# Tying the late weight conversions on VectorE behind the sum that precedes them in the program

## The chip, the cores and the metric

The kernel runs on one core of a Trainium2 chip. The metric is the device time of one execution in microseconds. The kernel before takes 1346.18 us, the median of three runs (1344.56 to 1347.51).

## What is computed

An attention over 4 batches, 12 heads, 448 positions and 64 channels, with an RMS norm on queries and keys, is followed by two feed-forward layers over the 1792 tokens that come out of it (768 wide, 2048 hidden). All weights arrive as float64.

```python
attn = softmax(rmsnorm(q, g_q) @ rmsnorm(k, g_k).T / sqrt(64)) @ v   # per batch and head
x = attn.transpose(0, 2, 1, 3).reshape(1792, 768)
h = x @ w_in;   r = max(h, 0);  x = (s * (r * r) + b) @ w_out         # layer 0
h = x @ w_in2;  g = h * cos(h); out = g @ w_out2                      # layer 1
```

## The kernel before

Every product of the layers is made of three TensorE products of float32 halves, so each operand is split into a high and a low part (`halves`, lines 379 to 383: ACT copies the high part, GpSimd or VectorE subtracts it).

The work runs in stages. Attention, pair of heads by pair of heads, runs beside layer 0 for the first two batches. Then come three passes over the hidden width, each in eight steps p: the pass (0,1) is layer 0 for the last two batches, the passes (1,0) and (1,1) are layer 1 for the first and the last two. A step has a `phase_in` (seven products of a Strassen scheme, with sums on VectorE at lines 767 and 772) and a `phase_out` (six output tiles of `unit_out_1` in layer 0, seven of `unit_out_2` in layer 1). An output tile is accumulated over the steps: its first visit is a copy on ACT (lines 530 and 554), each later one a VectorE sum of PSUM into the accumulator (lines 532 and 556). In the pass (0,1) `phase_out` of p stands in the program behind `phase_in` of p + 1, and so in the other passes.

`convert` (lines 385 to 413) turns one 128 x 384 block of float64 weights into float32: a DMA loads the raw block (lines 393 and 396, tile `raw`, two buffers), ACT makes `c` (line 402, two buffers) and `t` (line 403, three buffers), VectorE runs three operations in the order of the program: L406 puts the sign into `t`, L407 clips `c`, L408 joins both. For all but one kind of weight a DMA then stores the block (line 411, `wd`), and `prepare_in` and `prepare_out` load it from there and split it when its step comes.

The 64 blocks of layer 1 are the late ones (`late=True`). The last loop of the kernel places them: beside the steps of the passes (0,1) and (1,0) it adds to a credit, and at each whole credit one conversion is written into the program.

```python
            if calm:
                conversion(5.8 / 13 if q_ == passes[0] else 5 / 14)
```

The place in the program is not the place on an engine. The framework's scheduler lists each engine's instructions: it takes what is ready by its own model of time, the earlier one in the program first, and each engine then runs its list in order. A DMA is issued by SP in the order of its list as well. `issue_after(later, earlier)` adds an edge within one engine: the later instruction is listed behind the earlier one. It adds no semaphore.

Of the kernel before, what the change touches and what calls it, by code (L numbers as in the profile page):

```python
# [15 lines left out]
ALU = mybir.AluOpType  # L16
# [17 lines left out]
def body(ctx, tc, q, k, v, g_q, g_k, w1_in, w1_out, s_in, b_in, w2_in, w2_out, out):  # L34
    nc = tc.nc
# [43 lines left out]
    marks = {}  # L79
# [5 lines left out]
    def issue_after(later, earlier):  # L85
        info = mybir.DependencyInfo(mybir.DependencyClass.NoSync, mybir.DependencyReason.DATA)
        tc.add_manual_dep(later.ins, earlier.ins.name, info, reason="issue order")
# [12 lines left out]
    def products(w, x):  # L100
        return ((w[0], x[0]), (w[1], x[0]), (w[0], x[1]))
# [268 lines left out]
    def tile_of(ck, f):  # L370
        return ck + NCK * f
# [13 lines left out]
    def convert(layer, kind, a, e, o, gate=None, late=False):  # L385
        w = ((w1_in, w1_out), (w2_in, w2_out))[layer][kind]
        kk = f"{layer}_{kind}_{a}_{e}_{o}"
        own = late or count["raw"] % 3 < 2
        raw = (wp if own else pools["att"]).tile([P, CW], I64, tag="raw", name=f"raw_{kk}", bufs=2 if own else 1)
        count["raw"] += 1  # L390
        if kind == 0:
            src = w[o * CW:(o + 1) * CW, a * P:(a + 1) * P].rearrange("(c p) f -> p c f", p=P)
            dma = nc.sync.dma_start(raw.rearrange("p (c f) -> p c f", f=P), src)
        else:
            ft = tile_of(a, o)
            dma = nc.sync.dma_start(raw, w[ft * P:(ft + 1) * P, e * CW:(e + 1) * CW])
        ru = raw.bitcast(U32).rearrange("p (n two) -> p n two", two=2)
        lo, hi = ru[:, :, 0], ru[:, :, 1]
        c = wp.tile([P, CW], U32, tag="c", name=f"c_{kk}", bufs=2)
        cf = c.bitcast(F32)  # L400
        t = wp.tile([P, CW], U32, tag="t", name=f"t_{kk}", bufs=3)
        for z in (nc.scalar.activation(cf, hi.bitcast(F32), AF.Copy, scale=2.0**-112),  # L402
                  nc.scalar.activation(t, lo, AF.Copy, scale=LSCALE, bias=-0.5)):  # L403
            if gate is not None:
                issue_after(z, gate)
        nc.vector.scalar_tensor_tensor(t, hi, 0x80000000, t, ALU.bitwise_and, ALU.bitwise_or)  # L406
        nc.vector.tensor_scalar(cf, cf, VMAX, -VMAX, ALU.min, ALU.max)  # L407
        nc.vector.scalar_tensor_tensor(t, c, 3, t, ALU.logical_shift_left, ALU.bitwise_or)  # L408
        if (layer, kind) != (0, 1):
            d = dram.tile([P, CW], F32, tag=f"w_{kk}", name=f"wd_{kk}")  # L410
            nc.sync.dma_start(d, t.bitcast(F32))
            plain[layer, kind, a, e, o] = d
        return dma, t.bitcast(F32)
# [95 lines left out]
    def po_tile(key):  # L509
        if "psb" in pools:  # L510
            return pools["psb"].tile([P, 2, 512], F32, tag="po", name=f"po_{key}", bufs=2)
        return pools["psm"].tile([P, 512], F32, tag="mo", name=f"po_{key}", bufs=2)

    def unit_out_1(w, ck, et, bs):
        key = f"0_{ck}_{et}_{bs[0]}_{len(bs)}"
        cols = slice(et % (NE // 2) * P, (et % (NE // 2) + 1) * P)
        pr = bs[0] // 2
        po = po_tile(key)
        po = po[:, :len(bs), :S] if "psb" in pools else po[:, :S].unsqueeze(1)
        for k, b in enumerate(bs):  # L520
            for f in range(CF):
                for n, (a, m) in enumerate(products([z[:, cols] for z in w[f]], g[tile_of(ck, f), b])):
                    nc.tensor.matmul(po[:, k, :], a, m, start=(f == 0 and n == 0), stop=(f == CF - 1 and n == 2))  # L523
            visits[et, b] = visits.get((et, b), 0) + 1
        if (0, pr) not in acc:
            acc[0, pr] = ac.tile([P, 2 * NE * S], F32, tag="acc", name=f"acc_0_{pr}")
        n = (2 * et + bs[0] % 2) * S
        at = acc[0, pr][:, n:n + len(bs) * S].rearrange("p (k s) -> p k s", s=S)
        if visits[et, bs[0]] == 1:
            nc.scalar.copy(at, po)  # L530
            return
        nc.vector.tensor_tensor(at, po, at, ALU.add)  # L532
        if visits[et, bs[0]] < NCK:
            return
        for k, b in enumerate(bs):
            t = dram.tile([P, S], F32, tag=f"y_{b}_{et}", name=f"yd_{b}_{et}")
            nc.sync.dma_start(t, at[:, k, :])
            stash[1, b, et] = t

    def unit_out_2(w, pr, ck, t):  # L540
        key = f"1_{ck}_{pr}_{t}"
        j0 = t * P
        po = po_tile(key)[:, :, :EH]
        for eh in range(2):
            for f in range(CF):
                x = [z[:, j0:j0 + P] for z in g[tile_of(ck, f), "pair", pr]]
                for n, (a, m) in enumerate(products(x, w[eh][f])):
                    nc.tensor.matmul(po[:, eh, :], a, m, start=(f == 0 and n == 0), stop=(f == CF - 1 and n == 2))  # L548
        if (1, pr) not in acc:
            acc[1, pr] = ac.tile([P, NT * E], F32, tag="acc", name=f"acc_1_{pr}")  # L550
        rows_at = acc[1, pr][:, t * E:(t + 1) * E]
        at = rows_at.rearrange("p (k e) -> p k e", k=2)
        if ck == 0:
            nc.scalar.copy(at, po)
        else:
            nc.vector.tensor_tensor(at, po, at, ALU.add)  # L556
        if ck < NCK - 1:
            return
        j = j0
        while j < j0 + P:  # L560
            b, c, p = 2 * pr + j // S, j % S // CP, j % CP
            n = min(CP - p, j0 + P - j)
            rows = out[b * S:(b + 1) * S, :].rearrange("(p c) e -> c p e", c=NCH)[c, p:p + n, :]
            nc.sync.dma_start(rows, rows_at[j - j0:j - j0 + n, :])
            j += n
# [177 lines left out]
    def phase_in(layer, pr, p):  # L743
        w, x = late_w["in", layer, pr, p], late_x[layer, pr]
        key = f"{layer}_{pr}_{p}"
        pairs = []
        for f in range(CF):
            n = count["g"]
            count["g"] += 1
            gp, nb = (ma, 3) if n % 4 < 3 else (pools["lt"], 1)  # L750
            pairs.append([gp.tile([P, 2, S], F32R, tag=f"g{z}", name=f"g{z}_{key}_{f}", bufs=nb) for z in "hl"])
            for b in range(2):
                g[tile_of(p, f), 2 * pr + b] = [z[:, b, :] for z in pairs[f]]
            g[tile_of(p, f), "pair", pr] = [z.rearrange("p b s -> p (b s)") for z in pairs[f]]

        def bank(what):
            return pools["psb"].tile([P, 512], F32, tag="ph", name=f"ph_{key}_{what}", bufs=4)[:, :S]

        def product(at, a, b, first):
            wb = [z.rearrange("p (c f) -> p c f", f=P) for z in w[a]]  # L760
            for c in range(NE // 2):
                for n, (z, m) in enumerate(products([z[:, c, :] for z in wb], x[b, c])):
                    nc.tensor.matmul(at, z, m, start=(first and c == 0 and n == 0), stop=(c == NE // 2 - 1 and n == 2), skip_group_check=not first)  # L763

        def combine(what, at, u):
            t = temp("u", f"{what}_{key}", 3)
            nc.vector.tensor_tensor(t, at, u, ALU.add)
            return t

        def result(f, b, h, u=None, into=None):  # L770
            if u is not None:
                nc.vector.tensor_tensor(into, h, u, ALU.add)
                h = into
            epilogue_in_bank(layer, f"{key}_{f}_{b}", h, *(z[:, b, :] for z in pairs[f]))

        pa = bank("a")
        product(pa, "11", "11", True)
        p1 = temp("u", f"p1_{key}", 3)
        nc.scalar.copy(p1, pa)
        yield  # L780
        pb = bank("b")
        product(pb, "s2", "2", True)
        u2 = combine("u2", pb, p1)
        yield
        product(pa, "12", "21", False)
        result(0, 0, pa)
        yield
        pc = bank("c")
        product(pc, "s3", "3", True)
        u3 = combine("u3", pc, u2)  # L790
        yield
        pd = bank("d")
        product(pd, "s1", "1", True)
        result(1, 1, pd, u3, pb)
        yield
        product(pc, "22", "4", False)
        result(1, 0, pc, u2, pc)
        yield
        product(pd, "s4", "22", False)
        result(0, 1, pd, u2, pd)  # L800
        yield
# [132 lines left out]
```

## Time and profile before

| | |
|---|---|
| median of three runs | 1346.18 us |
| the profiled execution | 1347.68 us, span 1345.7 us |
| mean granted TensorE clock | 0.973 |
| busy: PE, DVE, ACT, POOL | 91%, 73%, 58%, 43% of the span |
| sums L532 into two banks at once, pass (0,1) | first start 688.1 us, last 878.6 us |
| sums L556, first of the pass (1,0) | 943.0 us |

PE is TensorE's matmuls, DVE is VectorE, POOL is GpSimd, SP issues the DMAs. The busy times are shares of the whole span. A stretch view gives them for one stage, with the granted clock. In a timeline the bracket tells how long the engine was idle before and what released it.

### The profile page before, as it was taken

How to read it: one execution, taken by the hardware profiler on the slowest of the kernel's cores; microseconds unless marked ns; L12 is line 12 of the kernel's file. 1: busy time of each engine (PE TensorE's matmuls, PEld its weight loads, DVE VectorE, ACT ScalarE, POOL GpSimd, SP SyncE). 2: the span in 40 equal slices, each digit the busy share in tenths (PEclk: the TensorE clock that was granted, in tenths of full speed). 3: DMA queues.
4: the chain of work that ended last, by engine and by line, in shares of the span. 5: the costliest groups of instructions: out<-in, count | busy, mean ns of one | idle time of the engine just before them, and what ended most of it. 6: DMA issues, size and time to landing. Idle time of an engine off the chain costs nothing.

```text
span 1345.7 us, 19429 instructions
## 1 busy us (share of the span) xinstructions
PE 1229.1 (91%) x6408; PEld 1008.1 (75%) x6408; DVE 978.1 (73%) x1539; ACT 784.6 (58%) x1749; POOL 578.7 (43%) x647
## 2 busy tenths in 40 slices
PE   5999998989899899865988989979999989999998
PEld 2555665767667676754877779869999979999998
DVE  5889769677767765899778886675766785576665
ACT  4778767655566554535766666457655653754451
POOL 3566538443353431465333335545655641111120
PEclk9999999999999899987999999989999989999999
DMA  3323325534343331776776775374444537433432
GB/s 103 111 85 122 118 74 184 160 117 138 107 157 105 105 108 57 238 278 207 245 228 229 247 243 185 131 253 153 171 158 135 189 96 233 149 124 106 130 118 82
DMA packets 152068, 207.83 MB, mean 154 GB/s; under 512 B 15872, under 2 KB 141984, under 8 KB 151968
## 3 DMA queue, kind: packets, MB, share of 16 engines
q1 hardware_dynamic: 151968, 206.60, 47.9%
q8 instruction: 50, 0.82, 0.3%
q14 instruction: 50, 0.41, 0.1%
HBM read 139.30 MB, written 67.24 MB: 153 GB/s over the span
## 4 chain that ended last, share of the span: by engine, by line
PE 47%; DVE 20%; ACT 11%; DMA 10%; issue 6%; POOL 5%; SPq 0%; POOLq 0%; ACTq 0%; DVEq 0%
PE po L548 15%; PE po L523 8%; DMA raw<-in_moe_w_in_dram 5%; DVE t L406 5%; PE ph_a L763 4%; ACT pr L230 4%; PE av L271 3%; PE ph_c L763 3%; PE sc L210 3%; PE ph_d L763 3%; PE ph L494 2%; DVE t L408 2%; PE ph_b L763 2%; PE tp L248 2%; DMA raw<-in_moe_w_out_dram 2%
## 5 line engine op out<-in xcount | busy, mean ns | idle before, releaser
L383 POOL TENSOR_TENSOR wl_o<-wl_o,wh_o 128x384 fp32r<-128x384 f32 x64 | 68.0, 1074 | 241.8 <-ACT wh_o L380 241.8
L548 PE MATMUL po<-wh_o,gh 128*128 128x384 f32 x448 | 151.9, 339 | 6.5 <-DVE acc L556 6.3
L230 ACT ACTIVATE pr<-sc,top 112x448 f32<-112x448 f32 x184 | 116.2, 634 | 69.6 <-DVE top L222 69.3
L548 PE MATMUL po<-wh_o,gl 128*128 128x384 f32 x448 | 150.6, 336 | 0.0
L548 PE MATMUL po<-wl_o,gh 128*128 128x384 f32 x448 | 148.5, 336 | 0.0
L556 DVE TENSOR_TENSOR acc<-po,acc 128x768 f32<-128x768 f32 x98 | 93.4, 954 | 55.0 <-PE po L548 54.8
L402 ACT ACTIVATE c<-raw 128x384 f32<-128x384 f32 x128 | 71.3, 557 | 101.7 <-DMA raw<-in_moe_w_in_dram 41.6
L248 PEld LDWEIGHTS tp<-ident,pr 112*112 112x112 f32 x768 | 78.5, 134 | 69.5 <-issue 13.4
L222 DVE TENSOR_REDUCE top<-sc 112x1 f32<-112x448 f32 x192 | 112.8, 616 | 23.7 <-PE sc L210 22.9
L532 DVE TENSOR_TENSOR acc<-po,acc 128x448 f32<-128x448 f32 (+1 forms) x126 | 97.0, 773 | 38.0 <-PE po L523 37.6
L406 DVE SCALAR_TENSOR_TENSOR t<-raw,t 128x384 uint32<-128x384 uint32 x128 | 103.6, 810 | 26.1 <-ACT t L403 23.9
L407 DVE TENSOR_SCALAR c<-c 128x384 f32<-128x384 f32 x128 | 69.6, 545 | 64.0 <-ACT c L402 63.6
L248 PE MATMUL tp<-ident,pr 112*112 112x112 f32 x768 | 102.6, 266 | 13.2 <-ACT pT L254 5.3
L210 PE MATMUL sc<-kT,qT 64*112 64x448 f32 x384 | 99.4, 595 | 0.9 <-DVE kT L201 0.9
L523 PE MATMUL po<-gh,wh_o 128*128 128x448 f32 x192 | 73.8, 386 | 25.5 <-DVE acc L532 13.7
L383 POOL TENSOR_TENSOR wl<-t,wh 128x384 fp32r<-128x384 f32 x64 | 68.4, 1076 | 61.8 <-ACT wh L380 60.5
L408 DVE SCALAR_TENSOR_TENSOR t<-c,t 128x384 uint32<-128x384 uint32 x128 | 92.5, 726 | 1.9
L548 PEld LDWEIGHTS po<-wh_o,gh 128*128 128x128 f32 x448 | 84.6, 189 | 10.4 <-DVE acc L556 8.9
L523 PE MATMUL po<-gh,wh 128*128 128x448 f32 x192 | 77.6, 405 | 11.7 <-ACT r L459 7.4
L548 PEld LDWEIGHTS po<-wh_o,gl 128*128 128x128 f32 x448 | 84.7, 189 | 1.4
L548 PEld LDWEIGHTS po<-wl_o,gh 128*128 128x128 f32 x448 | 84.5, 189 | 0.4
L271 PE MATMUL av<-pT,rawv 112*64 112x448 f32 x384 | 79.5, 548 | 0.2 <-DVE pT L252 0.2
(175 smaller groups left out, 3480.3 us busy)
## 6 DMA issues: line engine op xcount, KB each, us to landing
raw<-in_moe_w_in_dram SPq DMA_DIRECT2D x64, 384.0 KB, 3.7
raw<-in_moe_w_out_dram SPq DMA_DIRECT2D x64, 384.0 KB, 3.4
wd<-t SPq DMA_DIRECT2D x96, 192.0 KB, 3.6
wl_o<-wd SPq DMA_DIRECT2D x64, 192.0 KB, 2.4
rd<-wh SPq DMA_DIRECT2D x56, 192.0 KB, 1.9
rd<-wl SPq DMA_DIRECT2D x56, 192.0 KB, 1.9
wl<-wd SPq DMA_DIRECT2D x48, 192.0 KB, 3.2
wh_o<-rd SPq DMA_DIRECT2D x32, 192.0 KB, 3.8
```

The costliest lines, as they stand in the source:

```text
L210: mm.append(nc.tensor.matmul(sc[j], st[i]["qT"][half, c * CP:(c + 1) * CP], st[i]["kT"][half, :], start=True, stop=True))
L222: line("DVE", nc.vector.tensor_reduce(tops[j], sc[j], axis=AX.X, op=ALU.max, negate=True))
L230: e = line("ACT", nc.scalar.activation(pr, sc[j], AF.Exp, bias=tops[j], scale=scale[j], accum_out=st[i]["sums"][:, c, j:j + 1]))
L248: mm = [nc.tensor.transpose(tp[:, kc * CP:(kc + 1) * CP], pr[:, kc * CP:(kc + 1) * CP], ident[:CP, :CP]) for kc in range(NCH)]
L271: mm.append(nc.tensor.matmul(st[i]["pa"][j * D:(j + 1) * D, :], st[i]["v"][:, j, kc, :], st[i]["pT", j][:, kc, :], start=(kc == 0), stop=( ...
L383: eng.tensor_tensor(wl, w, wh.bitcast(F32), ALU.subtract)
L406: nc.vector.scalar_tensor_tensor(t, hi, 0x80000000, t, ALU.bitwise_and, ALU.bitwise_or)
L408: nc.vector.scalar_tensor_tensor(t, c, 3, t, ALU.logical_shift_left, ALU.bitwise_or)
L523: nc.tensor.matmul(po[:, k, :], a, m, start=(f == 0 and n == 0), stop=(f == CF - 1 and n == 2))
L532: nc.vector.tensor_tensor(at, po, at, ALU.add)
L548: nc.tensor.matmul(po[:, eh, :], a, m, start=(f == 0 and n == 0), stop=(f == CF - 1 and n == 2))
L763: nc.tensor.matmul(at, z, m, start=(first and c == 0 and n == 0), stop=(c == NE // 2 - 1 and n == 2), skip_group_check=not first)
```

## The change

A dictionary entry `marks["sum"]` holds the VectorE sum that the program wrote last: an accumulator sum (lines 532, 556) or a combination of the Strassen scheme (lines 767, 772). In a late conversion the first of the three VectorE operations, L406, is tied behind that sum. L407 is not tied; L408 needs the result of L406. The DMA, the two ACT operations, the rates and the numbers of buffers stay.

```diff
-        nc.vector.scalar_tensor_tensor(t, hi, 0x80000000, t, ALU.bitwise_and, ALU.bitwise_or)
+        z = nc.vector.scalar_tensor_tensor(t, hi, 0x80000000, t, ALU.bitwise_and, ALU.bitwise_or)
+        if late:
+            issue_after(z, marks["sum"])
...
-        nc.vector.tensor_tensor(at, po, at, ALU.add)
+        marks["sum"] = nc.vector.tensor_tensor(at, po, at, ALU.add)
...
-            nc.vector.tensor_tensor(at, po, at, ALU.add)
+            marks["sum"] = nc.vector.tensor_tensor(at, po, at, ALU.add)
...
-            nc.vector.tensor_tensor(t, at, u, ALU.add)
+            marks["sum"] = nc.vector.tensor_tensor(t, at, u, ALU.add)
...
-                nc.vector.tensor_tensor(into, h, u, ALU.add)
+                marks["sum"] = nc.vector.tensor_tensor(into, h, u, ALU.add)
```

## Rows read from the trace of the kernel before

**Rows 1.** Single lines, late stretches: count, min/median/max ns, first and last start.

```profile
L406 DVE SCALAR_TENSOR_TENSOR t<-raw,t x64: 542/559/1509, 551.9 to 808.0; 128x384 uint32<-128x384 uint32 x64
L556 DVE TENSOR_TENSOR acc<-po,acc x41: 943/950/959, 943.0 to 1108.6; 128x768 f32<-128x768 f32 x41
```

**Rows 2.** Stretches: length, busy (count) of PE, PEld, DVE, ACT, POOL; clock, DMA, GB/s.

```profile
587.00:640.00 53.00, 25.81 (x76) 20.62 (x75) 49.07 (x59) 29.20 (x63) 36.33 (x30) 0.68 0.67 214
640.00:810.00 170.00, 152.03 (x709) 133.93 (x708) 139.60 (x214) 110.38 (x227) 63.95 (x55) 0.98 0.74 237
900.00:1070.00 170.00, 166.40 (x878) 157.43 (x877) 114.18 (x167) 105.41 (x207) 96.09 (x93) 1.00 0.46 156
```

**Rows 3.** What PE waited for from 551 to 640 us: total, times, longest.

```profile
PE po L523 <- DMA wh_o<-rd: 10.3, 1, 10.3
PE ph_b L763 <- ACT wh_s L380: 6.4, 1, 6.4
PE ph_c L763 <- DVE u_u L767: 5.9, 1, 5.9
PE po L523 <- ACT r L459: 4.5, 1, 4.5
```

**Rows 4.** Timeline of DVE from 593 us: start, duration, instruction.

```profile
593.54 1.16 DVE L407 TENSOR_SCALAR c<-c 128x384 f32<-128x384 f32 x1
...
600.79 1.41 DVE L677 TENSOR_TENSOR xr<-xl,xr 128x448 f32<-128x448 f32 x1
```

**Rows 5.** Groups on DVE from 587 to 640 us: count, busy us, mean ns, idle before.

```profile
L406 DVE SCALAR_TENSOR_TENSOR t<-raw,t 128x384 uint32<-128x384 uint32 x10 | 9.5, 953 | 0.2
L408 DVE SCALAR_TENSOR_TENSOR t<-c,t 128x384 uint32<-128x384 uint32 x10 | 8.2, 829 | 0.2
L407 DVE TENSOR_SCALAR c<-c 128x384 f32<-128x384 f32 x10 | 7.8, 777 | 2.9 <-ACT c L402 2.9
```

**Rows 6.** Timeline of ACT from 561 us.

```profile
561.20 0.54 ACT L402 ACTIVATE c<-raw 128x384 f32<-128x384 f32 x1 [1.97 <-DMA raw<-in_moe_w_in_dram]
561.64 0.53 ACT L459 ACTIVATE r<-ph 128x448 f32<-128x448 f32 x1
```

**Rows 7.** Stretches of one step each: two of pass (0,1), two of pass (1,0).

```profile
655.00:689.00 34.00, 29.27 (x139) 25.44 (x138) 25.49 (x40) 26.46 (x54) 13.38 (x12) 1.00 0.78 240
756.00:789.00 33.00, 29.77 (x135) 26.03 (x134) 27.90 (x45) 20.53 (x44) 13.03 (x12) 0.95 0.78 251
...
943.00:971.00 28.00, 27.34 (x146) 25.88 (x145) 19.52 (x30) 16.44 (x33) 15.38 (x16) 1.00 0.43 146
999.00:1028.00 29.00, 28.45 (x152) 26.97 (x152) 19.93 (x30) 17.07 (x33) 15.99 (x16) 1.00 0.45 151
```

**Rows 8.** Who waited from 640 to 810 us: DVE for ACT, PE for DVE.

```profile
DVE c L407 <- ACT c L402: 27.6, 26, 3.6
PE po L523 <- DVE acc L532: 11.6, 7, 2.8
```

**Rows 9.** Groups on DVE from 640 to 870 us.

```profile
L532 DVE TENSOR_TENSOR acc<-po,acc 128x896 f32<-128x896 f32 x39 | 42.2, 1084 | 10.0 <-PE po L523 10.0
L406 DVE SCALAR_TENSOR_TENSOR t<-raw,t 128x384 uint32<-128x384 uint32 x48 | 36.5, 761 | 1.5
L408 DVE SCALAR_TENSOR_TENSOR t<-c,t 128x384 uint32<-128x384 uint32 x48 | 34.3, 718 | 0.8
L407 DVE TENSOR_SCALAR c<-c 128x384 f32<-128x384 f32 x48 | 25.9, 539 | 27.8 <-ACT c L402 27.6
```

**Rows 10.** Timeline of DVE from 804 us: one conversion with GpSimd idle.

```profile
804.13 0.36 DVE L407 TENSOR_SCALAR c<-c 128x384 f32<-128x384 f32 x1 [0.65 <-ACT c L402]
804.57 0.56 DVE L406 SCALAR_TENSOR_TENSOR t<-raw,t 128x384 uint32<-128x384 uint32 x1
805.17 0.56 DVE L408 SCALAR_TENSOR_TENSOR t<-c,t 128x384 uint32<-128x384 uint32 x1
```

**Rows 11.** DMA issues: count, KB each, median us from issue to landing.

```profile
wd<-t SPq DMA_DIRECT2D x96, 192.0 KB, 3.6
wl<-wd SPq DMA_DIRECT2D x48, 192.0 KB, 3.2
```

**Rows 12.** A GpSimd line in pass (1,0), 900 to 1070 us: min/median/max ns.

```profile
L383 POOL TENSOR_TENSOR wl<-wl,wh x18: 997/1030/1487, 915.4 to 1061.6; 128x384 fp32r<-128x384 f32 x18
```

## The prediction

> **What bounds the kernel now.** I read first when the late conversions run. The code asks for 78 steps of the pass (0,1) at 5.8/13 and 84 of the pass (1,0) at 5/14, so 34 and 30 of the 64 conversions, the last of them written behind sums of L556. The single-line view shows all 64 between 551.9 and 808.0 us, and the first L556 only at 943.0 [rows 1]. The scheduler has pulled every one of them far ahead of the sum that precedes it in the program. So the tie is no fine ordering: it moves all 64, and 30 of them into another pass.
>
> Then the stretches. At the start of the pass (0,1), 587 to 640 us, PE is busy 25.8 us of 53, at a clock of 0.68 of full speed, while DVE is busy 49.1 [rows 2]. From 640 to 810 PE is idle for 18.0 us of 170, DVE busy for 139.6. From 900 to 1070 PE is busy for 166.4 of 170 and DVE for 114.2. Conversions sit where DVE is the tight engine and are absent where PE is.
>
> **The change, part by part.**
>
> *The start of the pass (0,1).* Ten conversions leave the stretch of 587 to 640 us. Their three instructions take 953 + 829 + 777 = 2559 ns on average there, 25.5 us together, half of what DVE does [rows 5]. They stand ahead of work that PE needs: from 593.54 to 600.79 two conversions run before the subtraction L677 that makes an operand [rows 4], and PE then waits 5.9 us for the combination L767; of its other waits, 6.4 us end with ACT's copy of a weight part and 10.3 us with a weight load [rows 3]. SP has the raw loads of these conversions in the same list, each held until L406 of two conversions earlier frees a raw buffer, and the weight loads stand behind them. All of that goes. What is late next is GpSimd: 36.3 us busy in the 53 [rows 2], so this stretch can hardly fall below 36.3, a gain of at most 16.7. At the least only the wait for the DVE combination goes: 5.9. The chain through DVE is close to full here (49.1 of 53), so I take the upper end, 16.
>
> A little earlier ACT stands still at L402 for a raw block, and L459, which PE waits for (4.5 us), runs only behind it [rows 6, 3]. Only two raw buffers exist, so from the third conversion on no load is sent before the first tied L406 has run, and that L402 is no longer there: 4. Both places together: 20 us less, bounds 6 and 21.
>
> *The rest of the pass (0,1).* A step of it takes 33 to 34 us, with PE busy 29.3 to 29.8 and DVE 25.5 to 27.9 [rows 7]. From 640 to 810 DVE also stands still for 27.6 us at L407, in wait for ACT and, behind ACT, for a raw block, and every sum queued behind waits along; PE loses 11.6 us to sums L532 [rows 8]. Afterwards a step holds 5.8 conversions instead of 48 / 170 x 33.5 = 9.5, at 761 + 718 + 539 = 2018 ns each [rows 9]; DVE has 7.5 us less to do per step, the sum goes before its conversion, and the inputs of the next two conversions are loaded while the tie holds them, so L407 finds its data. A sum L532 (1084 ns, one per output tile) can still find one conversion in front of it. I take the 11.6 us as gone, 12 in all; bounds 0 and the whole idle time of 18.0.
>
> *The pass (1,0).* It gets 30 conversions, five to a step. DVE is busy 19.5 and 19.9 us in steps of 28 and 29 us, where PE has hardly a gap (27.3 and 28.5 busy) [rows 7]. What a conversion costs there no row shows, since none runs there now. With GpSimd idle it takes 0.36 + 0.56 + 0.56 = 1.48 us [rows 10]; at a GpSimd share of 64.0 / 170 = 38% it took 2.02 us [rows 2, 9], at 36.3 / 53 = 69% 2.56 us [rows 2, 5]. From 900 to 1070 GpSimd is busy 96.1 / 170 = 57% [rows 2], between the two: 2.02 + 19/31 x 0.54 = 2.35 us. A step then asks DVE for 19.7 + 5 x 2.35 = 31.5 us in a mean of 28.5. DVE becomes the bound by 3.0 us a step: 18 us over six steps. With 1.48 a step asks for 27.1 and all is hidden: 0. With 2.56 it is 32.5: 24 us. I take 18, the value by interpolation. The cover that hides the conversions in this pass is DVE's idle time, and it is used up.
>
> On who pays for the meeting of DVE and GpSimd: L406 lies between 542 and 1509 ns [rows 1], and a GpSimd subtraction between 997 and 1487 [rows 12], so each of the two is stretched at times. The Trainium skill, "SBUF — State Buffer", section "Who interferes with whom", says that a VectorE instruction with two SBUF inputs and a GpSimd instruction that reads SBUF exclude each other, and that the one that issues second waits until the first is done. The stretched rows agree with it. By that rule it isn't given that DVE pays: if the tied conversions start first, GpSimd waits instead, and the sum would be 0 for this pass where the rows give 18. This is the second rival.
>
> *The weights that come last.* The steps of p = 7 need blocks whose conversion is among the last eight. From the tied sum on, a block needs its conversion (1.48 to 2.56), a store (3.6) and a load (3.2) [rows 11], 8 to 9 us, before GpSimd and ACT can split it. Now these blocks lie ready since 808 us. Bounds 0 and one such chain, 9; I take 2, since five of six steps have their blocks a step ahead.
>
> *What costs nothing.* ACT's two operations and the transfers move along with their conversion; ACT is busy 105.4 us and the DMA 46% from 900 to 1070 [rows 2]. If a raw load has to wait for a late L406, SP holds the weight loads behind it; that is part of the first rival. Behind L406 in DVE's list stand L408 and the next sums; who waits for those is PE, with two accumulator buffers.
>
> The sum: -20 - 12 + 18 + 2 = -12 us against the profiled execution, 1347.7 (span 1345.7), so 1335.7. That execution lies 1.5 us above the median of 1346.2; against the median the forecast is 1334 us.
>
> **The rivals.**
>
> *Slower: the pass (1,0) takes over the blocked queue.* Place: DVE's list from 890 to 1070 us. In the pass (0,1) DVE was not only busy, it stood still 27.6 us of 170 behind conversions [rows 8], 5.4 us in a step of 33.5. If the same comes with the conversions, because ACT and SP, in order as well, deliver a raw block late to a DVE that is full, a step takes 31.5 + 5.4 = 36.9 us, 8.4 more than now: 50 us. Then -20 - 12 + 50 + 2 = +20: 1366 us. It decides the sign from steps of 28.5 + 30 / 6 = 33.5 us on. For it speaks that DVE is asked for more than it has; against it that the tie lets two raw blocks arrive ahead.
>
> *Faster still: the conversions slip into gaps.* If they meet GpSimd rarely or start first, a step stays at PE's own length: -20 - 12 = -32, 1314 us. For it: DVE is idle for about 9 us in each step, and 7.4 would do.
>
> *The start of the pass (0,1) doesn't shorten.* If the weight load (10.3 us) and the weight part (6.4 us) of [rows 3] are late for reasons of their own, only the 5.9 us go: -6 - 12 + 18 + 2 = +2, 1348 us, no measurable change.
>
> *The tie does nothing.* It would, were the sums listed first already. They are not [rows 1].
>
> **How the numbers follow.** Forecast 41%, slower rival 26%, faster rival 20%, unshortened start 11%, no effect 2%. A difference under 0.2%, 2.7 us, can't be told from no change. Faster by more: nearly all of the forecast and of the faster rival and a little of the third, 62%. Slower by more: the first rival and a few of the third and of the forecast's own bounds, 29%. Within: 9%. The forecast's own bounds run from -21 - 18 + 0 + 0 = -39 (1307) to -6 + 0 + 24 + 9 = +27 (1373), with its middle at 1320 to 1346. For eight times in ten I leave out the ends of both: 1308 to 1362 us, which takes in the faster rival and the milder half of the slower one.
>
> **What would show it.** L406 is seen up to about 1060 us, and none from 560 to 640. DVE is busy about 24 us less from 587 to 640, PE's waits for L767 and for the weight load are gone there, and L407 hardly waits for ACT. From 900 to 1070 DVE is near 95% busy, a step takes about 31 us, and PE waits for sums L556. Wrong would be: steps above 33.5 us there (slower rival), steps of 28.5 (faster rival), or a start as long as now.

## The result and the profile after

The changed kernel takes 1329.14 us, the median of four runs (1328.22 to 1330.63), beside 1346.03 us for the kernel before (1344.56 to 1347.51). The ratio is 0.9876 with a 95% interval of 0.9859 to 0.9893: 17 us faster. The forecast was 1334 us, and the range held the time. Three of the sum's four terms came out at nearly their size, the fourth was too small, and the mechanism behind two of them (the fourth, and the one for the pass (1,0)) was not, or not wholly, the one that I had given. Behind the change line numbers are two higher: L407 is L409, L408 is L410, L532 is L534, L556 is L558, L767 is L769.

The profiled execution took 1328.91 us. Its page and the single-line view of the late L406 (the columns of [rows 1]):

```profile
span 1327.0 us, 19412 instructions
PE 1229.2 (93%) x6408; PEld 1008.5 (76%) x6408; DVE 971.2 (73%) x1539; ACT 782.4 (59%) x1749; POOL 584.4 (44%) x647
...
L406 DVE SCALAR_TENSOR_TENSOR t<-raw,t x64: 543/550/1377, 623.0 to 1048.0; 128x384 uint32<-128x384 uint32 x64
```

DVE's share of the span is the 73% of before, yet 64 conversions that ran in 256 us [rows 1] are now spread over 425. The stretches that answer to [rows 2], with its columns:

```profile
587.00:640.00 53.00, 42.78 (x173) 37.35 (x174) 34.52 (x44) 31.08 (x64) 39.71 (x34) 0.84 0.45 140
640.00:810.00 170.00, 165.56 (x802) 149.17 (x801) 126.39 (x187) 105.00 (x213) 70.87 (x63) 1.00 0.66 208
900.00:1070.00 170.00, 154.99 (x777) 142.91 (x777) 150.47 (x223) 110.60 (x230) 103.21 (x89) 0.97 0.68 222
850.00:1060.00 210.00, 186.06 (x931) 171.82 (x930) 180.47 (x276) 143.74 (x294) 118.56 (x105) 0.95 0.70 230
```

In the two stretches of the pass (0,1) PE does 17.0 and 13.5 us more in the same time, and its clock is higher. In the pass (1,0) it does 11.4 us less, and its clock falls from 1.00 to 0.97. That is the shape of the forecast: a gain in one pass, part of it given back in the next.

A fixed window compares different work, since the program has moved in time. So I matched the instructions of the two kernels by name and took, for each step, the end of the last matmul of the product d of its `phase_in`. The differences to before, in us (negative is earlier), for the points where a term of the sum ends:

| point (time before) | after | what lies since the point above | forecast |
|---|---|---|---|
| (0,1) p = 1 (654.4) | -19.4 | start: -19.4 | -20 |
| (1,0) p = 0 (890.0) | -39.0 | rest of pass (0,1): -19.6 | -12 |
| (1,0) p = 6 (1055.3) | -20.7 | pass (1,0): +18.3 | +18 |
| (1,1) p = 7 (1312.9) | -18.8 | last weights and the end: +1.9 | +2 |

What PE waited for: from 551 to 640 us, then from 640 to 810 us, then from 850 to 1060 us (waited for, total, times, longest).

```profile
PE po L525 <- DVE acc L534: 6.1, 3, 2.6
PE ph_a L765 <- ACT u_p L781: 5.9, 1, 5.9
PE ph_a L765 <- DVE gl L485: 3.1, 1, 3.1
...
PE po L525 <- DVE acc L534: 2.2, 3, 1.5
PE ph_c L765 <- DVE u_u L769: 1.5, 1, 1.5
...
PE ph_a L765 <- DVE gl L485: 7.8, 1, 7.8
PE po L550 <- DVE acc L558: 7.8, 4, 3.3
PE po L550 <- ACT wh_o L380: 4.2, 3, 1.9
```

At the start the four waits of [rows 3], 27.1 us, are gone but for 0.6; shorter ones have come in their place. From 640 to 810 us the wait for accumulator sums fell from 11.6 us [rows 8] to 2.2. From 850 on sums and weight parts hold PE up. (The single wait of 7.8 us for `gl` is where the passes change; the same wait was 6.5 us in the kernel before.)

How the conversions stand in the pass (1,0): groups on DVE from 850 to 1050 us (columns as in [rows 5]) and waits of ACT, of SP and of DVE from 850 to 1060 us.

```profile
L406 DVE SCALAR_TENSOR_TENSOR t<-raw,t 128x384 uint32<-128x384 uint32 x30 | 22.9, 765 | 0.2
L410 DVE SCALAR_TENSOR_TENSOR t<-c,t 128x384 uint32<-128x384 uint32 x29 | 21.9, 756 | 0.1
L409 DVE TENSOR_SCALAR c<-c 128x384 f32<-128x384 f32 x28 | 15.2, 544 | 6.2 <-ACT c L402 6.0
...
ACT c L402 <- DMA raw<-in_moe_w_out_dram: 12.1, 6, 3.9
ACT c L402 <- DMA raw<-in_moe_w_in_dram: 5.9, 6, 1.5
ACT t L403 <- DMA raw<-in_moe_w_out_dram: 4.8, 2, 2.8
...
SPq L396 <- DVE t L406: 15.2, 10, 3.8
SPq L393 <- DVE t L406: 4.6, 5, 1.6
...
DVE gt L479 <- ACT kk L477: 11.9, 10, 3.3
```

A conversion costs 765 + 756 + 544 = 2065 ns there, less than the 2.35 us that I had worked out. DVE is busy for 150.5 of 170 us (89%), or 180.5 of 210 (86%): loaded, not full. What the busy share doesn't show is that SP, ACT and DVE, each in its own order, stand still around one raw block. The timelines of SP, DVE and ACT around 990 us show one turn of it (start, duration, instruction, idle before and what ended it):

```profile
988.74 0.33 SPq L396 DMA_DIRECT2D raw<-in_moe_w_out_dram  x1
990.63 0.45 SPq L741 DMA_DIRECT2D wl_o<-wd  x1
...
988.17 0.55 DVE L406 SCALAR_TENSOR_TENSOR t<-raw,t 128x384 uint32<-128x384 uint32 x1
990.50 0.62 DVE L480 SCALAR_TENSOR_TENSOR gt<-kk,gt 128x448 f32<-128x448 f32 x1
992.51 0.36 DVE L409 TENSOR_SCALAR c<-c 128x384 f32<-128x384 f32 x1 [0.86 <-ACT c L402]
...
991.93 0.55 ACT L402 ACTIVATE c<-raw 128x384 f32<-128x384 f32 x1 [3.87 <-DMA raw<-in_moe_w_out_dram]
992.82 0.56 ACT L481 ACTIVATE gt<-gt 128x448 f32<-128x448 f32 x1
```

The tied L406 at 988.17 frees a raw buffer, and only then SP sends the next raw load. That lands 3 us later; ACT has stood still for 3.87 us at its L402. Behind L402 stands L481, a step of layer 1's nonlinearity whose input DVE had finished about 1.7 us before, and DVE in turn stands at L409. So the tie, by holding L406, also holds the next raw load. I had counted only the other side of this: that two loaded blocks wait ready behind the tie.

### The profile page after: what moved, and what is told of

The parts are those of the page before. It is cut to its first block, busy times and chain, and to the rows that moved or that the text cites. A ratio compares the mean times of both kernels' runs of the same rounds, so it can differ in the third digit from the quotient of the medians.

```text
span 1327.0 us, 19412 instructions
## 1 busy us (share of the span) xinstructions
PE 1229.2 (93%) x6408; PEld 1008.5 (76%) x6408; DVE 971.2 (73%) x1539; ACT 782.4 (59%) x1749; POOL 584.4 (44%) x647
## 4 chain that ended last, share of the span: by engine, by line
PE 44%; DVE 19%; ACT 13%; DMA 13%; issue 5%; POOL 4%; SPq 1%; ACTq 0%; POOLq 0%; DVEq 0%
PE po L550 12%; PE po L525 7%; DMA raw<-in_moe_w_in_dram 5%; PE ph_a L765 4%; DVE t L406 4%; ACT pr L230 4%; PE av L271 3%; PE ph L496 3%; PE sc L210 3%; DMA raw<-in_moe_w_out_dram 3%; PE ph_c L765 3%; PE ph_d L765 3%; PE tp L248 2%; DVE t L410 2%; DVE acc L534 2%
## 5 line engine op out<-in xcount | busy, mean ns | idle before, releaser
L402 ACT ACTIVATE c<-raw 128x384 f32<-128x384 f32 x128 | 71.1, 555 | 114.2 <-DMA raw<-in_moe_w_out_dram 44.8
L222 DVE TENSOR_REDUCE top<-sc 112x1 f32<-112x448 f32 x192 | 112.9, 616 | 23.7 <-PE sc L210 22.9
L534 DVE TENSOR_TENSOR acc<-po,acc 128x448 f32<-128x448 f32 (+1 forms) x126 | 97.0, 773 | 35.8 <-PE po L525 35.5
L558 DVE TENSOR_TENSOR acc<-po,acc 128x768 f32<-128x768 f32 x98 | 93.3, 952 | 40.4 <-PE po L550 40.1
L409 DVE TENSOR_SCALAR c<-c 128x384 f32<-128x384 f32 x128 | 68.6, 538 | 73.9 <-ACT c L402 73.3
L406 DVE SCALAR_TENSOR_TENSOR t<-raw,t 128x384 uint32<-128x384 uint32 x128 | 99.7, 781 | 24.2 <-ACT t L403 23.3
L410 DVE SCALAR_TENSOR_TENSOR t<-c,t 128x384 uint32<-128x384 uint32 x128 | 96.0, 752 | 1.4
L525 PE MATMUL po<-gh,wh 128*128 128x448 f32 x192 | 77.4, 404 | 13.5 <-DVE acc L534 9.6
L403 ACT ACTIVATE t<-raw 128x384 uint32<-128x384 uint32 x128 | 70.5, 550 | 19.3 <-POOL wl L383 11.1
```

Of the source, the lines that this page charges most:

```text
L222: line("DVE", nc.vector.tensor_reduce(tops[j], sc[j], axis=AX.X, op=ALU.max, negate=True))
L406: z = nc.vector.scalar_tensor_tensor(t, hi, 0x80000000, t, ALU.bitwise_and, ALU.bitwise_or)
L534: marks["sum"] = nc.vector.tensor_tensor(at, po, at, ALU.add)
```

## The experiments

Edits are shown against the changed kernel. This table holds for all of them the same points as above, as differences to the kernel before in us, beside the median time.

| kernel | median us | (0,1) p = 1 | (1,0) p = 0 | (1,0) p = 6 | end |
|---|---|---|---|---|---|
| the change | 1329.14 | -19.4 | -39.0 | -20.7 | -18.8 |
| start_only | 1347.77 | -7.4 | +0.2 | +0.1 | -0.4 |
| first34 | 1329.47 | -19.2 | -27.1 | -17.3 | -18.5 |
| last30 | 1349.42 | +0.5 | -19.2 | +4.5 | +3.8 |
| noclip | 1322.73 | -18.5 | -43.3 | -30.0 | -25.4 |
| rate45 | 1335.34 | -16.3 | -18.6 | -11.4 | -11.5 |
| clip_tied | 1331.01 | -18.8 | -34.5 | -17.0 | -16.7 |
| xr7 | 1331.70 | -22.5 | -38.0 | -20.6 | -22.5 |
| raw3 | 1322.95 | -22.0 | -37.5 | -30.1 | -26.4 |
| raw3_noclip | 1319.90 | -19.4 | -43.0 | -33.2 | -31.6 |
| raw3_untied | 1337.69 | -2.8 | -14.9 | -15.1 | -11.8 |
| raw3_xr5 | 1334.24 | -20.4 | -36.4 | -19.1 | -15.6 |
| raw3_ct | 1328.35 | -17.7 | -37.6 | -17.1 | -21.0 |

The points come from one profiled execution of each kernel, so a difference of 2 or 3 us in them is not much. The medians decide. Behind each median below stands its ratio to the kernel before, measured beside it, with a 95% interval. Four kernels scatter more widely than the others: start_only and last30 over some 11 us, rate45 over 12 us, clip_tied over 5 us with one run 9 us above the rest.

### Where the gain comes from: out of the way, or spread

**start_only** ties all 64 conversions behind one sum alone, the first combination of the pass (0,1). None can run before it, and nothing paces them afterwards.

```diff
-            issue_after(z, marks["sum"])
+            issue_after(z, marks["first"])
...
             marks["sum"] = nc.vector.tensor_tensor(t, at, u, ALU.add)
+            marks.setdefault("first", marks["sum"])
```

> All 64 late conversions are tied behind one sum alone, the first combination of the pass (0,1), and are free after it. Theory (what counts is where the conversions run): the start of the pass (0,1) keeps its gain of 20 us, the rest of that pass is as crowded as in the kernel before (0 to +5 us), the pass (1,0) has none: about 1328 us, 1322 to 1334. Rival (what counts is that each sum stands ahead of its conversion): most of the gain is gone, 1340 to 1346 us.

Measured: 1347.77 us, ratio 1.0008 (0.9987 to 1.0029). The theory missed by 20 us, and even the rival's 1340 to 1346 us, with most of the gain gone, lie under it. The single-line view, the first stretch for L406 alone (length, DVE's busy time (count), clock, DMA, GB/s) and the first two stretches:

```profile
L406 DVE SCALAR_TENSOR_TENSOR t<-raw,t x64: 540/558/1381, 603.3 to 826.2; 128x384 uint32<-128x384 uint32 x64
...
587.00:640.00 53.00, 8.19 (x11) 0.74 0.69 215
...
587.00:640.00 53.00, 34.65 (x122) 28.56 (x123) 44.53 (x59) 27.39 (x58) 31.37 (x25) 0.74 0.69 215
640.00:810.00 170.00, 149.78 (x692) 130.41 (x692) 139.49 (x216) 110.41 (x226) 63.26 (x55) 0.98 0.75 237
```

The conversions begin 51 us later than before and end 18 us later, in 223 us instead of 256. That first combination ran at 603 us, so the edit didn't empty the start: 11 conversions stand between 587 and 640 us, as many as before (10, [rows 5]); in the change there are 4. DVE does as much from 640 to 810 us as before (139.5, [rows 2]). Only 7.4 us are won at the start, and by p = 7 they are lost. So holding the first conversions back is not the gain as long as all of them follow at once. What an emptied start alone is worth, with a dense rest behind it, no run tells.

**first34** and **last30** tie one part each: the 34 of the pass (0,1), or the 30 of the pass (1,0).

```diff
-        if late:
+        count["late"] += late
+        if late and count["late"] <= 34:
```

(`> 34` in last30; `count` gets an entry `"late": 0`.)

> Only the 34 conversions that the program places in the pass (0,1) are tied; the other 30 are free and run as soon as buffers allow, from about 790 us on. Theory: up to 790 us all as in the changed kernel (about 40 us ahead of the kernel before), then 30 dense conversions cost the end of the pass (0,1) and the start of the pass (1,0) 10 to 25 us, and the pass (1,0) loses less than the 18 us of the changed kernel: 1316 to 1330 us, 1322 likeliest. Rival (a conversion costs 0.6 us of the total wherever it runs): 1329 us as changed.

> Only the 30 conversions that the program places in the pass (1,0) are tied; the first 34 are free as in the kernel before and done by about 705 us. Theory: the start of the pass (0,1) gains nothing, the stretch from 710 us on gains about 10 us, the pass (1,0) costs 18 us: 1354 us, 1346 to 1362. Rival (the 30 ties bring a part of the gain wherever the other conversions run): at or under 1337 us.

Measured: first34 1329.47 us (0.9862, 0.9835 to 0.989), last30 1349.42 us (1.0009, 0.999 to 1.0028). Their late L406 in turn:

```profile
L406 DVE SCALAR_TENSOR_TENSOR t<-raw,t x64: 541/548/1380, 623.2 to 949.6; 128x384 uint32<-128x384 uint32 x64
...
L406 DVE SCALAR_TENSOR_TENSOR t<-raw,t x64: 541/558/1498, 552.1 to 1071.4; 128x384 uint32<-128x384 uint32 x64
```

first34 lies at the rival's 1329 us, which is also the edge of the theory's range; last30 came within its theory. All that the change gains comes from the first 34. In first34 the other 30, free but behind the tied ones in the order of the raw loads, run together until 949.6: from (0,1) p = 6 (-36.8) to (1,0) p = 3 (-13.1) they cost 23.7 us, and 5 of these come back by the end. Tied or free, these 30 cost the same by the medians. In last30 the first 34 run at once from 552 us on and spoil the start as before; the pass then wins 20 us after 654, because only 34 conversions are left in it, and the 30 tied ones cost 23.7 in the pass (1,0).

**rate45** writes 45 conversions into the pass (0,1) and 19 into the pass (1,0), all tied.

```diff
-                conversion(5.8 / 13 if q_ == passes[0] else 5 / 14)
+                conversion(7.5 / 13 if q_ == passes[0] else 3.4 / 14)
```

> The changed kernel with the two rates at 7.5/13 and 3.4/14, so that the program places 45 late conversions in the pass (0,1) and 19 in the pass (1,0), instead of 34 and 30. Theory (at 34 the pass (0,1) loses almost nothing to conversions, in the pass (1,0) each costs about 0.6 us): 11 x 0.6 = 7 us less than the changed kernel, less some 2 us as VectorE fills up in the pass (0,1): 1324 us, 1321 to 1327. Rival (a conversion costs the same in either pass): 1329 us.

Measured: 1335.34 us, 0.9918 (0.9893 to 0.9942). The expectation had the sign wrong. The stretch from 640 to 810 us, and PE's first wait in it:

```profile
640.00:810.00 170.00, 157.19 (x742) 139.36 (x743) 135.79 (x199) 104.80 (x217) 72.39 (x63) 0.99 0.69 215
...
PE po L525 <- DVE acc L534: 8.1, 8, 2.3
```

The tie is that of the change, sum first, and still PE waits for sums again (8.1 us against 2.2) and is idle for 12.8 us against 4.4. The rest of the pass (0,1) gains 2.3 us instead of 19.6: eleven conversions more cost 17 us there, 1.6 us each. The pass (1,0) pays 7.2 us for 19 instead of 18.3 for 30. In both passes of this one trace the price of one more rises with those that are there: the rival, one price wherever a conversion runs, missed as well.

### What the pass (1,0) pays for: DVE's time or standing still

**noclip** leaves the clip (L409) out of the late conversions, a quarter of their time on DVE.

```diff
-        nc.vector.tensor_scalar(cf, cf, VMAX, -VMAX, ALU.min, ALU.max)
+        if not late:
+            nc.vector.tensor_scalar(cf, cf, VMAX, -VMAX, ALU.min, ALU.max)
```

> The changed kernel, with the clip (the second of the three VectorE operations) left out of the 64 late conversions; the sizes of these weights never reach the bound. VectorE has 64 x 0.54 = 34 us less to do, 16 us of them in the pass (1,0). Theory (VectorE's load is what the pass (1,0) pays for): the 18 us of that pass fall to about 4, the pass (0,1) stays: 1315 us, 1310 to 1320. Rival (the pass pays for queues that stand still behind late raw blocks): the third operation waits for ACT instead of the clip, 1325 to 1329 us.

Measured: 1322.73 us, 0.9816 (0.9796 to 0.9837), 6.4 us under the change and between the ranges of theory and rival. Two thirds of it come in the pass (0,1), which ends 4.3 us earlier. From (1,0) p = 0 to p = 6 the kernel gives back 43.3 - 30.0 = 13.3 us instead of 18.3, and to the end 17.9 instead of 20.2, with DVE busy 144.0 of the 170 us from 900 on instead of 150.5. Up to p = 6 DVE is busy 11 us less than in the change (142.8 against 154.1), and the price of the pass falls by 2 to 5 us, where the theory of a full DVE wanted 14.

**clip_tied** ties the clip as well, so that DVE doesn't reach it before its sum.

```diff
             issue_after(z, marks["sum"])
+            issue_after(y, marks["sum"])   # y: the clip
```

> The changed kernel with the clip (the second VectorE operation) tied behind the same sum as the first. VectorE stood still 31.7 us at that clip between 640 and 800 us. Theory (TensorE lost only some 4 us in that stretch, so the standing still costs little): that wait shrinks by half or more and the time stays, 1327 to 1331 us. Rival (what VectorE loses there is lost to the end): 1322 us or less.

Measured: 1331.01 us, 0.9902 (0.9871 to 0.9932). DVE's wait for ACT at the clip from 640 to 810 us, of the change and of clip_tied (the clip is at L407 there):

```profile
DVE c L409 <- ACT c L402: 32.4, 21, 3.2
...
DVE c L407 <- ACT c L402: 10.1, 5, 3.3
```

Two thirds of the wait go and no time with them. So in the changed kernel, with its conversions spread, less of this standing wins the pass (0,1) nothing (15.7 us behind p = 1 instead of 19.6). The kernel before was not tried so; raw3_untied below bears on it.

**raw3** gives the late raw blocks a third buffer, **xr7** is its comparison: the room comes from `xr`, seven buffers instead of nine.

```diff
+        if late and count["raw"] % 3 == 2:
+            raw = pools["lt"].tile([P, CW], I64, tag="raw", name=f"raw_{kk}", bufs=1)
+        else:
+            raw = ...   # as before: two buffers
...
-            return load(temp("xr", f"{layer}_{pr}_{what}_{c}", 9), b, c)
+            return load(temp("xr", f"{layer}_{pr}_{what}_{c}", 7), b, c)
```

> The changed kernel with 7 instead of 9 load buffers for the operands of the passes, and nothing else: the comparison for the kernel with a third raw buffer. Both theories: 1329 to 1336 us, by what later loads of the operands cost at the starts of the passes.

> The changed kernel with a third raw buffer for the late conversions; for its room the operands of the passes have 7 instead of 9 load buffers (the next kernel has that alone). Theory (in the pass (1,0) ACT stands still for raw blocks and SP behind raw loads that wait for the tied operation): SP's waits for that operation (20 us from 850 to 1060) and ACT's for raw blocks (23 us) fall to under 8 each, and the time is 5 to 12 us under that of the next kernel. Rival (the pass pays for VectorE's own work there): within 2 us of the next kernel.

Measured: xr7 1331.70 us, 0.9893 (0.9868 to 0.9919); raw3 1322.95 us, 0.9833 (0.9812 to 0.9855). The third buffer is worth 8.7 us by the medians. From 850 to 1060 us in raw3 (line numbers three higher than in the change), the stretch, then what PE, SP and ACT waited for; in between the stretch from (1,0) p = 0 to p = 6 by the points of the table, first of the change, then of raw3:

```profile
850.00:1060.00 210.00, 191.43 (x976) 177.88 (x975) 189.09 (x285) 148.34 (x300) 129.10 (x112) 0.97 0.71 236
...
851.00:1034.60 183.60, 163.07 (x819) 151.35 (x820) 154.07 (x243) 124.31 (x254) 95.59 (x86) 0.95 0.68 225
852.50:1025.20 172.70, 159.72 (x820) 149.01 (x821) 153.02 (x241) 125.22 (x253) 95.71 (x84) 0.97 0.72 239
...
PE po L553 <- DVE acc L561: 2.5, 1, 2.5
PE po L553 <- ACT wh_o L380: 0.5, 1, 0.5
...
SPq L399 <- DVE t L409: 10.6, 6, 3.7
SPq L396 <- DVE t L409: 6.2, 5, 1.8
...
ACT t L406 <- DMA wd<-t: 13.2, 15, 1.8
ACT c L405 <- DVE t L413: 11.7, 11, 2.3
```

PE's waits for sums and weight parts fall from 7.8 + 4.2 in the change (8.1 + 2.6 in xr7) to 2.5 + 0.5 us. Between the two points DVE does the same work as in the change, 153.0 us against 154.1, in 172.7 us instead of 183.6: DVE's load was not the bound there. Nor were the transfers by their load alone, with the DMA engines 72% busy in the faster kernel and 68% in the slower. SP still stands for 16.8 us behind tied L409s, where I had expected under 8. ACT no longer waits for raw blocks at all, 22.8 us in the change, but it now waits 24.9 us at the same place for a free `t` and a free `c`. So ACT's standing as such has not gone.

**raw3_noclip** joins the two edits, **raw3_untied** is raw3 without the tie.

> The kernel with a third raw buffer (and 7 load buffers for operands), with the clip left out of the 64 late conversions. With two raw buffers leaving the clip out brought 6 us, none of them in the middle of the pass (1,0). Theory (with the raw blocks on time, what is left of the cost of the pass (1,0), 11 us, is VectorE's own work): leaving out 30 x 0.54 = 16 us of it there takes most of the 11: 1314 us, 1310 to 1318. Rival (the rest comes from transfers and weights that land late): 1319 to 1323 us.

> The kernel with a third raw buffer (and 7 load buffers for operands), without the tie: the conversions are free as in the kernel before. Theory (the gain comes from spreading the conversions; without the tie a third buffer lets them run still denser and as early): no gain on the kernel before, 1342 to 1352 us. Rival (the kernel before paid for raw blocks that came late, and the tie was only one way around that): 1330 us or less.

Measured: raw3_noclip 1319.90 us, 0.9806 (0.9781 to 0.9831). The median lies in the rival's range, above the theory's, but the runs reach from 1317.61 to 1324.87. With the third buffer there, leaving out the clip gives 3 us by the medians, and the intervals of the two ratios overlap. What the pass (1,0) gives back from p = 0 on, to p = 6 and to the end:

| kernel | to p = 6 | to the end |
|---|---|---|
| the change | 18.3 | 20.2 |
| noclip | 13.3 | 17.9 |
| xr7 | 17.4 | 15.5 |
| raw3 | 7.4 | 11.1 |
| raw3_noclip | 9.8 | 11.4 |

By either column the third buffer lowers the price (by 10.0 and 4.4 us with the clip, 3.5 and 6.5 without it). The clip's time on DVE takes 5.0 and 2.3 us off it with two raw buffers and nothing with three.

raw3_untied: 1337.69 us, 0.9927 (0.9912 to 0.9941), between the two expectations. Its L409 behind 640 us (L406 of the kernel before), its stretch from 640 to 810 us, and there DVE's wait at the clip and PE's for sums:

```profile
L409 DVE SCALAR_TENSOR_TENSOR t<-raw,t x48: 544/558/1404, 640.0 to 778.8; 128x384 uint32<-128x384 uint32 x48
...
640.00:810.00 170.00, 158.25 (x747) 142.31 (x746) 139.90 (x221) 116.50 (x240) 70.82 (x63) 0.97 0.72 236
...
DVE c L410 <- ACT c L405: 6.9, 11, 1.7
...
PE po L526 <- DVE acc L535: 7.8, 3, 3.6
```

The third buffer (with seven for `xr`) is worth 9 us without any tie and with nothing won at the start (-2.8). Its conversions stand denser than in the kernel before: the 48 behind 640 us are done at 778.8 instead of 808.0 us [rows 1]. Yet the rest of the pass (0,1) gains 12.1 us; DVE is as busy as before but stands at the clip for 6.9 us instead of 27.6, and PE waits for sums for 7.8 us instead of 11.6 [rows 8]. So density alone is not the price either: a crowd whose raw blocks come late costs more than one whose blocks are there. The tie is worth 15 us on top of the buffer. raw3, which leaves nothing out, is faster than both kernels.

**raw3_ct** takes up ACT's waits: a third buffer for `c` and a fourth for `t` in the late conversions, with the room taken from `xr` (five buffers). **raw3_xr5** is raw3 with five, its comparison.

```diff
-        c = wp.tile([P, CW], U32, tag="c", name=f"c_{kk}", bufs=2)
+        third = late and count["raw"] % 3 == 0
+        c = (pools["lt"] if third else wp).tile([P, CW], U32, tag="c", name=f"c_{kk}", bufs=1 if third else 2)
...   # t in the same way: every fourth in "lt"
```

> The comparison for the next kernel: raw3 with five instead of seven buffers for xr, so that there is room for more. Both theories expect the time of raw3, 1322 to 1327 us; the loads of the token blocks may come later at the start of each pass, which would cost some us at most (xr7 against the change: 2.6 us, hardly outside the spread).

> raw3_xr5 with a third buffer for c and a fourth for t in the late conversions. In raw3 ACT's waits for raw blocks from 850 to 1060 us are gone, but it waits in front of the conversions for a free t (13.2 us, for the store of an earlier block) and for a free c (11.7 us, for DVE): 24.9 us, as much as the 22.8 us for raw blocks in the change. Theory: what is left of the price of the pass (1,0), 11 us, is ACT standing at conversions with the work of layer 1 behind it. Then these waits fall below 10 us and the time 4 to 8 us below raw3_xr5. Rival: ACT's standing was never the price; the raw loads that went out late were, and the rest is sums and weight parts that find DVE and the transfers occupied. Then the waits fall as well, and the time stays within 2 us of raw3_xr5.

Measured: raw3_xr5 1334.24 us, 0.991 (0.9896 to 0.9925); raw3_ct 1328.35 us, 0.9868 (0.985 to 0.9885). ACT's longest waits in raw3_ct from 850 to 1060 us:

```profile
ACT c L407 <- DMA raw<-in_moe_w_in_dram: 11.9, 8, 4.7
ACT c L407 <- DMA raw<-in_moe_w_out_dram: 9.6, 8, 2.6
```

The 5.9 us between the two have the size that the theory gave, but not its place: from (1,0) p = 0 to p = 6 raw3_ct gives back 20.5 us and raw3_xr5 17.3, and the gain comes only in the pass (1,1). The waits at `c` and `t` went as expected and came back as 21.5 us for raw blocks. With all its waits at these two operations ACT stands 25.6 us in front of conversions in the change, 24.9 in raw3, 25.2 in raw3_xr5 and 27.6 here, for whatever buffer is the scarcest, while the pass costs 18.3, 7.4, 17.3 and 20.5 us to p = 6. So the length of ACT's standing does not set the price. raw3_xr5 missed its expectation by 7 us: with two buffers of `xr` less the time is back at that of xr7 (1331.70 us, intervals that overlap).

## Why the prediction was right, and where it wasn't

**The start, 20 us: right.** 19.4 us came. No late L406 runs before 623 us and four before 640, the waits of [rows 3] for the weight load and the weight part are gone, and so is most of the rest. GpSimd is what is nearest to the length: 39.7 us busy of 53. DVE does 14.6 us less in the window, not 24: four conversions are left in it, and work from behind the old 640 us has moved into it. start_only doesn't test this term, since 11 conversions stayed in the stretch; of the parts of the reason (DVE's queue, the raw loads ahead of the weight loads) no run takes out one alone.

**The rest of the pass (0,1), 12 us: a term that was too small.** 19.6 us came, more than the 18.0 us of idle time that I had set as its upper bound. Two things failed. I counted only the 11.6 us that ended with sums L532, while PE's idle time from 640 to 810 us fell from 18.0 to 4.4 us, 13.6. And I left out the clock: it went from 0.98 [rows 2] to 1.00, by estimate another 0.02 x 170 = 3.4 us. Together that is 17.0 of this one window, and the pass goes on behind it to 890. The reason was half wrong as well. I said that L407 would find its data and that this would set DVE free. It still waits (32.4 us, against 27.6 in [rows 8]), and clip_tied shows that in the changed kernel less of this wait wins nothing. In the kernel before, where every conversion has the next close behind it, late raw blocks did cost something, as far as raw3_untied shows: it gains 12.1 us in this pass with no tie. What the tie takes away is the crowd, fewer conversions in the pass: first34 (17.6 us from p = 1 to p = 6, against 19.7), start_only (all of them at once: none) and rate45 (45 instead of 34: 2.3 us left of 19.6) show this.

**The pass (1,0), 18 us: right in size by luck, by another mechanism.** 18.3 us came. The mean step, from p = 0 to p = 6, went from (1055.3 - 890.0) / 6 = 27.6 us to 30.6, where I had 28.5 to 31.5. But the step that produced the 18 failed: DVE didn't become the bound. It was 86 to 89% busy where I had named 95%, and a conversion took 2.07 us where I had interpolated 2.35, though GpSimd was as busy as assumed (103 of 170 us, 61%; 57% assumed). By my own formula, 19.7 + 5 x 2.07 = 30.0 us of DVE in a step of 28.5, the loss would have been 9 us: a conversion taken too dear and waits left out made up for each other. noclip and raw3 deny the mechanism from both sides: 11 us less work on DVE lower the price by only 2 to 5 us, and with the third raw buffer the same work of DVE fits into 10.9 us less. The first rival's mechanism is there in a mild form: raw loads held by tied L406s, with ACT and SP in order behind them. I had argued it away with two blocks that arrive ahead. A third raw buffer lowers the price, yet raw3_ct shows that it isn't simply ACT's standing. Worked out from the starts of successive matmuls between the two points, PE has 23.0 us of gaps (more than 0.4 us from one start to the next, less the spacing at full clock) against 10.1 in the kernel before, and matmuls at the lower clock (0.37 us from start to start for 448 columns, instead of 0.21) make 4.8 us more than before: 12.9 + 4.8 = 17.7 of the 18.3. In raw3, which gives back 7.4 us, the gaps are 14.6 us and the matmuls at the lower clock make 2.1 us more.

**The last weights, 2 us: not decided.** Between p = 6 and the end 1.9 us more are lost, which is within what one execution scatters, and no wait at p = 7 can be named that is a late weight block. Waits for weight parts (`wh_o`, 4.2 us) are spread over the pass.

**The rivals.** The slower one named waits that are really there, but 50 us for them was almost three times the 18.3 that the whole pass cost. The faster one (GpSimd pays or meetings are rare) had something: L406 and L410 lie at 765 and 756 ns, between the 560 of a free one [rows 10] and the 953 of the crowded start [rows 5]. Its price was wrong, 18 us where it had 0. The exclusion that the Trainium skill states in "SBUF — State Buffer", section "Who interferes with whom", fits these rows as it fitted those before; by it the one that issues second waits, and no run here shows how often that was DVE. The third rival, 6 us at the start, is refuted by the 19.4 us, and the last one by the 64 conversions that moved.

**What stays open.** The price of the pass (1,0) is not settled. It is not DVE's busy time alone (noclip, raw3), not the length of ACT's standing at conversions (raw3, raw3_xr5, raw3_ct), not whether the 30 are tied (first34). It falls with their number (rate45) and with a third raw buffer, as long as `xr` keeps seven (raw3, raw3_xr5). Sums behind conversions, weight parts that arrive late and the lower clock behind each gap are seen in the traces of the change and of raw3, and no run parts them. Every edit of buffers also makes the scheduler list the instructions anew, and that was not held fixed; some of the 8.7 and of the 5.9 us may be that.

## What to carry to other kernels

Side work that only has to be done by some later time is paid by how densely it comes, and by how late its inputs are when it comes densely (raw3_untied): a scheduler that lists what is ready will crowd it, and an edge to the neighbouring instruction in the program is a cheap way to pace it. Such an edge holds not only its instruction but every buffer that this instruction frees, and with it the next load and all that stands in order behind that load, so try one more buffer at the head of the chain (here 8.7 us, while its room came from buffers that could be spared). Don't price an added load by the busy share of one engine alone: the pass that was to fill DVE slowed by 3 us a step with DVE at 86%.

## What the hardware showed

The clock was worth more than I had allowed. With few gaps TensorE ran at a granted 1.00 from 640 to 810 us, with the gaps of before at 0.98. In the pass (1,0), 12.9 us of gaps more came with 4.8 us more of matmuls at the lower level: more than a third as much again as the gaps themselves. The length of a conversion doesn't follow GpSimd's busy share alone: 2.07 us with GpSimd 55 to 61% busy (850 to 1050 and 900 to 1070 us), against 2.02 us with 38% and 2.56 us with 69% [rows 2, 5, 9]. That spread conversions meet GpSimd less often than crowded ones is my reading; no run varies that alone.
